# A fused attention and maxout kernel: the first weight pieces cut by column quarters, batch 1 loaded ahead of the weights, and zeros multiplied in the early waits of TensorE

## The chip, the cores and the metric

The kernel runs on one core of one Trainium2 chip. The metric is the device time of one execution in microseconds (us). The numbers used here are the median of the timed runs and the span, busy times and rows of one profiled execution.

## The reference

Two parts follow each other. In the first, tokens `x` (8 batches, 8 heads, 512 tokens, 64 wide) read a small state (32 rows for each batch and head) by softmax attention, and the state reads the tokens. In the second, the 544 result rows of each batch (all heads side by side, 512 wide) go through a maxout layer of width 1024 and back to 512.

```python
scores = scale * np.matmul(x, state.transpose(0, 1, 3, 2))      # scale = 1 / sqrt(64)
a = softmax(scores);   xread = np.matmul(a, state)
scores2 = scale * np.matmul(state, x.transpose(0, 1, 3, 2))
a2 = softmax(scores2); sread = np.matmul(a2, x)
x = concatenate([xread, sread], axis=2)   # rows of 512 = heads x 64
g = np.maximum(x @ w1, x @ w2)
return (g @ w_out).astype(np.float32)     # 4352 x 512
```

## The kernel before

The maxout is written as `max(h1, h2) = relu(h1 - h2) + h2`, so only two weight matrices are needed: `wd = W1 - W2` (512 x 1024) and `wwo = W2 @ Wo` (512 x 512). Since `xread` is attention times state, the state of a batch is multiplied into both first (`sw`), and the attention weights then work on the small products. All matmuls are in bf16. The output of a token block is `relu(at @ sw) @ Wo + at @ (state @ wwo)`.

The program has three stretches. A first stretch, written out by hand as a table of tokens (`ORDER`), loads everything that comes first, builds `wd` and `wwo`, and does batches 0 and 1 and the preparation of batch 2. A loop then does batches 2 to 6 and prepares the next one in each pass, and a tail does batch 7 and the rows of the state. A branch at the end, not taken for these inputs, holds a slower general form.

Each token of `ORDER` emits one helper's instructions, so the table fixes the order on every engine. The name stands for the helper; numbers are batch, half, piece or chunk; `@n` names the PSUM bank (there are eight), `>V`, `>A`, `>P` the engine: VectorE (DVE), ScalarE (ACT), GpSimd (POOL). Transfers are issued by SyncE's queue (SP), in the order of the table; only the first piece of the state goes through ScalarE's queue.

- `ldx.b.g` loads half of batch b's heads, `ldS` state, `ldw1.k` and `ldw2.k` piece k of W1 and W2 (512 KB each, `PIECES` gives its columns and rows), `ldwo.q` a quarter of Wo's rows (512 KB).
- `ce` casts a pair of heads to bf16 (L209), `xt` transposes half a batch on TensorE in 8 matmuls (L225), `xte` copies that out. `sc` is the scores (8 matmuls, L240), `exp` the exponential on ScalarE (L248), `red` the sums and their reciprocal, `mul` the normalised weights `a`, `at` their transpose (L267), `ate` its copy. `sr`, `sre`, `srt`, `srte` are the state's reading of the tokens (L280 to L299).
- `cS`, `S`, `Se` cast, transpose and copy the state of the first batches (`sbd`). `mS`, `Sd`, `cb`, `xtd`, `atd` do the same work for later batches with DMA transposes, which SyncE issues (L204, L218, L261).
- `cw2.k` casts a piece of W2, `w2.k` transposes it (8 matmuls, L405), `w2e.k` copies it out to `w2m`. `cwo.q` casts a quarter of Wo. `ww.i.q` adds two matmuls (L460) to row block i of `wwo`: it needs `w2e` of the columns 256q to 256q + 255 and `cwo.q`. `wwe.i` copies block i out.
- `sub.k.h` subtracts half a piece, giving `wd` (L417). `sw.b.z` multiplies the state of batch b into chunk z of `wd` (`CHUNKS`) or, for `w`, into `wwo`, 8 small matmuls into two banks (L309); `swe` copies each bank out.
- `l1.b.f` is one block of 128 of the 1024 columns, two matmuls (L332), `re` its relu. `l2.b.c.q` adds two matmuls of quarter q (L346), or of the state part for `o` (L341), to output chunk c; `le` copies the chunk out and `store` writes the batch.

`idle.9@0` puts nine matmuls of zeros (L426, tile `wz`) ahead of the first transposes. `RELEASE` is the order in which the loop takes the eight banks, six for one ring and two for the other. A token that uses a bank waits until the bank's last reader is done. Each engine works strictly in its own order.

Of the kernel before, what the change touches and what calls it, by code (L numbers as in the profile page):

```python
# [20 lines left out]
ORDER = """
ldx.0.0 ldS.0.1 idle.9@0 ldx.0.1 ldw2.2 ldw2.3 ldwo.3 ldw1.3 ldw1.2 ldS.1.2 ce.0.0>V ce.0.1>P ldx.1.1 cS.0.1>V ldx.1.0
S.0.1@0 xt.0.0@1 Se.0.1.0>V Se.0.1.1>A ce.0.2>P ce.0.3>A xte.0.0>V xt.0.1@0 ldwo.2 sc.0.0@1 xte.0.1>V exp.0.0>A
cw2.2>P ldw2.1 sc.0.1@0 red.0.0>V exp.0.1>A w2.2@1 mul.0.0>P cw2.3>A sr.0@0 red.0.1>V ldw2.0 mul.0.1>P sre.0>V w2.3@2
cwo.3>A ldwo.0 w2e.2>V srt.0@0 at.0.0@3 srte.0>A sub.3.0>V w2e.3>A ldwo.1 sub.3.1>V ldw1.0 ate.0.0>A ww.2.3@2
sub.2.0>V ldw1.1 at.0.1@1 cS.1.2>A ww.3.3@3 ww.1.3@0 sub.2.1>V ate.0.1>A ldS.2.8 S.1.2@4 sw.0.1@1,5 Se.1.2.1>V
ce.1.3>A Se.1.2.0>V ce.1.2>P sw.1.1@4,6 swe.0.1.1>V ww.0.3@7 swe.0.1.0>A swe.1.1.0>V xt.1.1@5 swe.1.1.1>A ce.1.1>P
l1.0.7@1 ce.1.0>A xte.1.1>V l1.0.4@6 l1.0.6@4 re.0.7>A re.0.4>V cwo.2>P xt.1.0@5 re.0.6>A sc.1.1@1 l1.0.5@6 xte.1.0>V  # L30
exp.1.1>A ww.3.2@3 re.0.5>A sc.1.0@1 red.1.1>V ww.1.2@0 exp.1.0>A ww.2.2@2 cw2.1>V ww.0.2@7 l2.0.1.2@1 mul.1.1>P
ldx.3.1 red.1.0>V w2.1@6 cw2.0>A l2.0.2.2@5 mul.1.0>P w2e.1>V l2.0.2.3@5 l2.0.1.3@1 cwo.0>V w2.0@6 at.1.1@4 ww.2.0@2
w2e.0>V ldx.2.1 ww.3.0@3 cwo.1>P ate.1.1>V ww.0.0@7 ww.1.0@0 sub.0.1>V ldx.2.0 ww.3.1@3 at.1.0@4 ldx.3.0 sub.0.0>V
ww.0.1@7 wwe.3>A ww.1.1@0 sub.1.1>P ate.1.0>V wwe.0>A ww.2.1@2 wwe.1>V l1.1.7@7 wwe.2>A sr.1@4 sub.1.0>V re.1.7>A
sw.0.w@2,0 sre.1>V sw.0.0@3,6 swe.0.w.1>A l1.1.5@7 swe.0.w.0>V l1.1.6@4 swe.0.0.1>A mS.1>P l1.1.4@0 re.1.5>A re.1.6>V
l2.0.0.2@6 re.1.4>A l2.0.1.o@1 swe.0.0.0>V ce.3.2>P sw.1.0@4,7 mS.0>A sw.1.w@3,0 ce.3.3>P swe.1.0.1>V l2.0.0.3@6
swe.1.w.1>A cb.3.1>P Sd l1.0.0@2 swe.1.0.0>V l1.0.1@7 swe.1.w.0>A re.0.0>V l2.0.3.2@4 cb.2.1>P re.0.1>A l2.0.2.o@5
l1.1.1@2 ce.3.0>P l2.0.1.0@1 re.1.1>V l1.0.2@7 cb.2.0>P l1.1.3@3 re.0.2>V l2.0.3.o@4 re.1.3>A ce.3.1>P xtd.2 l1.1.0@2
ce.2.1>P l2.0.3.0@4 re.1.0>A srt.1@3 l2.0.0.0@6 ldx.4.0 cb.3.0>P srte.1>V l1.0.3@2 l2.0.0.o@6 re.0.3>A ce.2.2>P
l2.0.3.3@4 xtd.3 l1.1.2@2 ce.2.0>P l2.0.1.1@1 re.1.2>A ce.2.3>P l2.1.3.2@3 le.0.1>V l2.1.3.3@3 l2.1.3.1@3 l2.1.3.0@3  # L40
l2.1.2.2@1 ldx.4.1 l2.1.0.o@2 sc.2.1@7 l2.0.3.1@4 exp.2.1>A sc.2.0@0 l2.0.0.1@6 exp.2.0>A red.2.1>V l2.1.0.0@2
le.0.3>A l2.1.0.3@2 red.2.0>V mul.2.1>P l2.1.0.2@2 l2.1.2.3@1 le.0.0>V l2.1.2.o@1 mul.2.0>P l2.1.0.1@2 l2.0.2.0@5
le.1.0>A atd.2 l2.1.2.1@1 l2.0.2.1@5 l2.1.3.o@3 le.0.2>A l2.1.2.0@1 le.1.3>V sw.2.1@5,2 store.0 le.1.2>A sw.2.0@6,4
swe.2.1.0>V sw.2.w@3,0 swe.2.1.1>A sr.2@1 swe.2.0.0>V l2.1.1.3@5 swe.2.w.1>A l2.1.1.o@5 sre.2>V swe.2.0.1>A l2.1.1.2@5
l2.1.1.1@5 swe.2.w.0>V srt.2@1 l2.1.1.0@5 srte.2>V le.1.1>A
"""
# [8 lines left out]
@with_exitstack
def kernel(
# [363 lines left out]
    def wo_cast(q, eng):  # L420
        copy(eng, wo[:, 2 * q:2 * q + 2, :], half("o", q // 2)[:, q % 2 * 2:q % 2 * 2 + 2, :])

    def idle(n, ring):
        p = bank(ring)
        for j in range(n):
            nc.tensor.matmul(p, wz[:, 0:128], wz, start=True, stop=True)  # L426
# [2 lines left out]
    nc.vector.memset(ones, 1.0)
# [244 lines left out]
```

## Time and profile before

| | us |
|---|---|
| median of 3 runs | 150.77 (150.74 to 151.8) |
| profiled execution, its own time | 150.94 |
| span of the profiled execution | 149.0 |
| TensorE busy in the span | 138.1 (93%) |
| VectorE, ScalarE, GpSimd busy | 83.3, 66.1, 53.0 |
| mean granted TensorE clock | 0.989 |

A row of the timeline gives start, duration, engine, line, operation, output and inputs, the number of merged instructions, and in brackets how long the engine had been idle and what ended that. Matmuls are pipelined, so a merged row's duration is longer than the distance to the next row's start; the price of a step is read from start to start. DMA rows show the issue on a queue (SPq), and the landing of a transfer shows in the first row that waited for it. Lines are those of the kernel before; in the changed kernel all lines from the table's end on are two higher.

### The profile page before, as it was taken

The page shows a single profiled execution, that of the slowest core. Times are in us where ns is not written, and L with a number is a line of the kernel's source. Part 1 is how long each engine was busy: PE and PEld are TensorE (multiplying, and loading weights), DVE is VectorE, ACT ScalarE, POOL GpSimd, SP SyncE. Part 2 cuts the span into 40 slices and gives each one's busy share as a digit, 9 for nine tenths or more (in the row PEclk, how much of TensorE's full clock was granted, in tenths as well). Part 3 has the DMA queues.
Part 4 walks back from the last instruction along what each step waited for, and adds up shares of the span by engine and source line. Part 5 has one row for each costly group of instructions (what it writes and reads, how often), then busy time and mean ns, then how long its engine had stood idle before and what let it go on. Part 6 is the DMA issues. An engine that isn't in the chain of part 4 may idle for free.

```text
span 149.0 us, 3067 instructions
## 1 busy us (share of the span) xinstructions
PE 138.1 (93%) x1205; PEld 68.9 (46%) x1224; DVE 83.3 (56%) x163; ACT 66.1 (44%) x120; POOL 53.0 (36%) x81
## 2 busy tenths in 40 slices
PE   6846979999999999999999999999999999999990
PEld 2435446434445445444544454454445344754460
DVE  3567876796415367583855485376637586640120
ACT  3258673387324557045632745181547135511100
POOL 4352147497913700735091437056500500000000
PEclk9987999999999999999999999999999999999999
DMA  4999999996996568986969598779306033302332
GB/s 137 255 396 362 370 387 378 283 342 93 189 246 200 106 248 297 129 208 230 235 145 290 234 114 189 264 282 145 70 31 255 7 66 141 145 0 96 115 140 80
DMA packets 36063, 29.44 MB, mean 198 GB/s; under 512 B 23120, under 2 KB 31568, under 8 KB 35152
## 3 DMA queue, kind: packets, MB, share of 16 engines
q1 hardware_dynamic: 35776, 29.17, 69.9%
q8 instruction: 10, 0.16, 0.4%
q10 hardware_dynamic: 272, 0.07, 0.2%
q14 instruction: 5, 0.04, 0.1%
HBM read 15.20 MB, written 8.91 MB: 162 GB/s over the span
## 4 chain that ended last, share of the span: by engine, by line
PE 81%; DMA 10%; SPq 3%; DVE 1%; issue 1%; POOL 1%; ACT 0%
PE bank L346 38%; PE bank L332 17%; PE bank L341 9%; DMA big<-in_moe_w_out_dram 7%; PE bank L309 4%; PE bank L460 3%; DMA big<-in_x_dram 3%; SPq L155 3%; PE bank L365 2%; PE bank L375 2%; PE bank L240 2%; PE bank L280 1%; PE bank L373 1%; DVE wd L417 1%; POOL wo L103 1%
## 5 line engine op out<-in xcount | busy, mean ns | idle before, releaser
L346 PE MATMUL bank<-wo,r 128*128 128x512 bf16 (+1 forms) x259 | 61.4, 372 | 0.5
L346 PEld LDWEIGHTS <-r 128*128 128x128 bf16 x264 | 25.4, 98 | 28.5 <-issue 0.3
L99 ACT COPY big<-bank 128x512 f32<-128x512 f32 (+1 forms) x17 | 9.7, 573 | 47.1 <-PE bank L346 47.1
L332 PE MATMUL bank<-at,sw 128*128 128x512 bf16 x126 | 30.0, 379 | 0.1
L256 POOL TENSOR_TENSOR a<-e,er 128x512 bf16<-128x512 bf16 x16 | 16.7, 1065 | 36.3 <-ACT e L248 16.0
L327 DVE TENSOR_SCALAR r<-bank 128x512 bf16<-128x512 f32 x29 | 20.0, 691 | 15.9 <-PE bank L332 15.5
L325 ACT ACTIVATE r<-bank 128x512 bf16<-128x512 f32 x35 | 21.2, 608 | 8.2 <-PE bank L332 8.0
L101 DVE CAST sw<-bank 128x512 bf16<-128x512 f32 x24 | 15.3, 685 | 9.4 <-PE bank L309 9.3
L103 POOL CAST xe<-big 128x512 bf16<-128x512 f32 x28 | 16.4, 620 | 10.0 <-DMA big<-in_x_dram 10.0
L332 PEld LDWEIGHTS <-sw 128*128 128x128 bf16 x128 | 12.0, 98 | 14.0 <-issue 0.2
L101 DVE COPY big<-bank 128x512 f32<-128x512 f32 (+1 forms) x16 | 10.5, 654 | 13.6 <-PE bank L346 11.2
L341 PE MATMUL bank<-sw,at 128*128 128x512 bf16 (+1 forms) x56 | 17.1, 372 | 0.3
L103 POOL CAST xb<-big 128x1024 bf16<-128x1024 f32 x12 | 12.3, 1041 | 12.1 <-issue 11.4
L252 DVE TENSOR_REDUCE sums<-e 128x16 f32<-128x512 bf16 x16 | 10.6, 664 | 4.5 <-ACT e L248 4.4
L99 ACT CAST sw<-bank 128x512 bf16<-128x512 f32 x24 | 12.7, 599 | 0.2
L248 ACT ACTIVATE e<-bank 128x512 bf16<-128x512 f32 x16 | 9.0, 595 | 4.9 <-PE bank L240 4.5
L460 PE MATMUL bank<-wo,w2m 128*128 128x512 bf16 x30 | 7.8, 379 | 1.9 <-ACT w2m L99 1.2
L341 PEld LDWEIGHTS <-at 128*128 128x128 bf16 x66 | 5.7, 97 | 5.3
L240 PEld LDWEIGHTS <-xt 128*128 128x128 bf16 x128 | 5.1, 98 | 2.6 <-DVE xt L101 0.7
L240 PE MATMUL bank<-sbd,xt 128*128 128x64 bf16 x128 | 5.5, 193 | 0.6 <-DVE xt L101 0.6
L309 PE MATMUL bank<-wd,sbd 64*32 64x512 bf16 x128 | 5.8, 382 | 0.3 <-DVE sbd L101 0.2
L101 DVE COPY w2m<-bank 128x1024 bf16<-128x1024 bf16 (+1 forms) x4 | 2.8, 689 | 5.1 <-PE bank L375 4.1
(71 smaller groups left out, 105.1 us busy)
## 6 DMA issues: line engine op xcount, KB each, us to landing
big<-in_x_dram SPq DMA_DIRECT2D x14, 512.0 KB, 5.1
out_dram<-big SPq DMA_DIRECT2D x7, 1024.0 KB, 6.0
big<-in_moe_w_dram SPq DMA_DIRECT2D x8, 512.0 KB, 10.2
...
```

The source lines that it names most:

```text
L99: nc.scalar.copy(o, i)
L101: nc.vector.tensor_copy(o, i)
L103: nc.gpsimd.tensor_copy(o, i)
L240: nc.tensor.matmul(pv[:, c, kk], xt_s[b % 2][:, c, k, :], sbd[:, b, k, :], start=(c == 0 and kk == 0), stop=(c == NC - 1 and kk == 1))
L256: (nc.gpsimd if eng == "P" else nc.vector).tensor_mul(e_view(a_s[b % 2], hh), e_view(e_s[b % 2], hh), er_s[b % 2][:, hh].unsqueeze(3).to_b ...
L309: nc.tensor.matmul(pg[g][32 * i:32 * i + 32, 0:n], sbd[64 * g:64 * g + 64, b, i, 32 * g:32 * g + 32], rhs, start=True, stop=True)
L325: nc.scalar.activation(out=o, in_=p, func=ACTF.Relu)
L327: nc.vector.tensor_scalar(o, p, scalar1=0.0, scalar2=None, op0=ALU.max)
L332: nc.tensor.matmul(p, sw_s[b % 3][:, g, f * 128:(f + 1) * 128], at_s[b % 3][:, g].rearrange("p c t -> p (c t)"), start=(g == 0), stop=(g = ...
L341: nc.tensor.matmul(p[:, lo:hi], at_s[b % 3][:, g, c, :], sw_s[b % 3][:, g, FF + lo:FF + hi], start=(start and g == 0), stop=(stop and g == 1))
L346: nc.tensor.matmul(p[:, lo:hi], r_s[b % 2][:, f, c * 128:(c + 1) * 128], wo[:, f, lo:hi], start=(start and j == 0), stop=(stop and j == le ...
L460: nc.tensor.matmul(p, w2t[:, f, i, :], wo[:, f, :], start=(first and f % 2 == 0), stop=(last and f % 2 == 1))
```

## The change

Four things change, and with them the whole table of the first stretch.

- `PIECES`: the first half of W1's and W2's columns is cut into two column quarters over all rows (256 columns, rows of 1 KB in DRAM) instead of two row halves over 512 columns (rows of 2 KB). The second half stays as it was. The second quarter (piece 1) is loaded first.
- `CHUNKS`: batch 0 multiplies its state into `wd` in three chunks (256, 256, 512) instead of two.
- Zeros: the nine of `idle.9` become 21 single matmuls of zeros (`fill.k`; 512 columns for k from 100 on, else 256), twelve ahead of the first transposes and nine between later steps.
- `RELEASE`: the loop takes the banks in another order.

```diff
-PIECES = [(0, 512, 0, 2), (0, 512, 2, 4), (512, 1024, 0, 2), (512, 1024, 2, 4)]
+PIECES = [(0, 256, 0, 4), (256, 512, 0, 4), (512, 1024, 0, 2), (512, 1024, 2, 4)]
-CHUNKS = [[(0, 512), (512, 1024)], [(0, 512), (512, 1024)]]
+CHUNKS = [[(0, 256), (256, 512), (512, 1024)], [(0, 512), (512, 1024)]]
 ORDER = """
-ldx.0.0 ldS.0.1 idle.9@0 ldx.0.1 ldw2.2 ldw2.3 ldwo.3 ldw1.3 ldw1.2 ldS.1.2 ce.0.0>V ce.0.1>P ldx.1.1 cS.0.1>V ldx.1.0
+ldx.0.0 ldS.0.1 fill.103@0 ldx.0.1 fill.106@1 ldS.1.2 fill.100@0 ldx.1.1 fill.111@1 ldx.1.0 fill.2@0 fill.13@1
...
-RELEASE = [7, 2, 6, 0, 4, 3, 1, 5]
+RELEASE = [2, 4, 6, 0, 3, 7, 5, 1]
...
-    def idle(n, ring):
+    def idle(n, ring, w=512):
         p = bank(ring)
         for j in range(n):
-            nc.tensor.matmul(p, wz[:, 0:128], wz, start=True, stop=True)
+            nc.tensor.matmul(p[:, 0:w], wz[:, 0:128], wz[:, 0:w], start=True, stop=True)
...
+        fill=lambda k, r: idle(1, r, 512 if k >= 100 else 256),
```

On SyncE's queue, at the program's start, the transfers stood in this order (`big` are ten buffers of 1 MB, `sf` is the state; batch 0 goes to `big0`, batch 1 to `big7`):

```order
L155 DMA big0_109<-in_x_dram 128x4x256 x2
L163 DMA big4_113<-in_moe_w2_dram 128x2x512 x2
L167 DMA big6_115<-in_moe_w_out_dram 128x2x512
L163 DMA big5_114<-in_moe_w1_dram 128x2x512 x2
L171 DMA sf0_81<-in_state_dram 128x2x64
L155 DMA big7_116<-in_x_dram 128x4x256 x2
L167 DMA big6_115<-in_moe_w_out_dram 128x2x512
L163 DMA big1_110<-in_moe_w2_dram 128x2x512 x2
L167 DMA big3_112<-in_moe_w_out_dram 128x2x512 x2
L163 DMA big2_111<-in_moe_w1_dram 128x2x512 x2
```

Now they stand so:

```order
L157 DMA big0_109<-in_x_dram 128x4x256 x2
L173 DMA sf0_81<-in_state_dram 128x2x64
L157 DMA big7_116<-in_x_dram 128x4x256 x2
L165 DMA big1_110<-in_moe_w2_dram 128x4x256
L165 DMA big2_111<-in_moe_w1_dram 128x4x256
L165 DMA big1_110<-in_moe_w2_dram 128x4x256
L165 DMA big4_113<-in_moe_w2_dram 128x2x512
L169 DMA big3_112<-in_moe_w_out_dram 128x2x512 x2
L165 DMA big2_111<-in_moe_w1_dram 128x4x256
L169 DMA big6_115<-in_moe_w_out_dram 128x2x512
L165 DMA big4_113<-in_moe_w2_dram 128x2x512
L169 DMA big6_115<-in_moe_w_out_dram 128x2x512
```

State and batch 1 moved ahead of all weights, W2's quarters of 256 columns come first among these, and the first piece of Wo (`big3`, here `wo.1`) moved from the third place of the weights to the fifth. W1's second half (`big5`), which was loaded early, now comes last, behind the rows shown.

On ScalarE's queue, from batch 0's second exponential on, stood before (`e` exponentials, `wb` and `wo` casts of weights, `w2m` the transposed W2, `at` transposed attention, `xe` casts of x, `sw` the chunk products):

```order
L248 ACTIVATE e0_91<-bank0_63 128x8x64
L99 CAST wb1_108<-big4_113 128x1024
L99 CAST wo0_77<-big6_115 128x1024
L99 COPY sread_t0_78<-bank0_63 128x4x32
L99 COPY w2m0_80<-bank2_65 128x4x256
L99 COPY at0_99<-bank3_66 128x512
L99 CAST sb0_82<-sf0_81 128x256
L99 COPY at0_99<-bank1_64 128x512
L99 CAST xe1_85<-big7_116 128x2x4x64
```

Now stands there, up to the copy out of bank 5, which the first `ww` step takes next:

```order
L250 ACTIVATE e0_91<-bank1_64 128x8x64
L101 CAST xe1_85<-big7_116 128x2x4x64
L101 COPY xt1_88<-bank3_66 128x4x256
L101 COPY xt1_88<-bank1_64 128x4x256
L250 ACTIVATE e1_92<-bank0_63 128x8x64
L250 ACTIVATE e1_92<-bank1_64 128x8x64
L101 COPY w2m0_80<-bank4_67 128x1024
L101 COPY at0_99<-bank0_63 128x512
L101 CAST sw0_102<-bank3_66 128x256
L101 CAST sw0_102<-bank4_67 128x256
L101 CAST wb0_107<-big4_113 128x1024
L101 COPY sread_t0_78<-bank5_68 128x4x32
```

Batch 1's copies and exponentials moved ahead of the first weight work, the copies of `xt` came over from VectorE, and the cast of the first Wo piece went from here to VectorE.

More of the change, by code (lines that the diff above doesn't have):

```diff
@@ L26 @@
[L26 to L45, printed above, removed]
+ldx.0.0 ldS.0.1 fill.103@0 ldx.0.1 fill.106@1 ldS.1.2 fill.100@0 ldx.1.1 fill.111@1 ldx.1.0 fill.2@0 fill.13@1
@@ new lines @@
+ldw1.3 sub.1.0>P fill.113@0 red.1.0>V sr.1@1 w2e.1>A at.0.1@0 at.0.0@2 ldS.2.8 cw2.0>P ate.0.1>A sre.1>V sw.0.1@4,3
+srt.0@5 fill.4@6 fill.10@7 swe.0.1.1>A ate.0.0>V mul.1.0>P swe.0.1.0>A w2.0@3 red.1.1>V cw2.3>A l1.0.2@4 srt.1@2
+l1.0.3@7 cwo.1>V srte.0>A w2.3@6 re.0.3>A mul.1.1>V ww.2.1@5 ww.0.1@1 cwo.0>P w2e.0>A srte.1>V at.1.1@7 ww.1.1@0
+re.0.2>V ww.3.1@2 ate.1.1>A at.1.0@4 sub.0.0>V ww.0.0@1 w2e.3>A ww.2.0@5 sub.0.1>V ww.3.0@2 ate.1.0>A ww.1.0@0 cwo.2>V
+sw.1.0@4,6 ldx.2.0 sw.0.0@7,3 ww.2.2@5 swe.1.0.1>A swe.1.0.0>V ww.3.2@2 swe.0.0.1>A cw2.2>V l1.1.0@4 l1.1.2@3
@@ new lines @@
+swe.0.0.0>V w2.2@6 cwo.3>A re.1.0>V ldx.2.1 l1.0.0@7 w2e.2>V l1.0.1@4 re.1.2>A ww.2.3@5 sub.2.0>V re.0.0>A l1.1.3@3
+ldx.3.1 ww.3.3@2 wwe.2>A re.0.1>V sub.2.1>P ww.0.3@1 ldx.3.0 wwe.3>A ww.0.2@1 sub.3.1>V ww.1.3@0 re.1.3>A ww.1.2@0
+sub.3.0>V wwe.0>A l1.1.1@3 mS.1>P wwe.1>A sw.0.2@1,2 re.1.1>V sw.1.1@4,5 swe.0.2.0>A sw.0.w@0,7 swe.0.2.1>V sw.1.w@3,6
+swe.1.1.1>A l2.0.0.0@1 swe.1.1.0>V l2.0.0.1@1 swe.0.w.0>A l1.0.7@5 swe.0.w.1>V mS.0>A l2.0.3.0@0 cb.2.0>P re.0.7>V
+l1.1.5@7 swe.1.w.1>A Sd l1.1.4@4 re.1.5>V ce.2.1>P l1.0.5@5 re.1.4>A l1.0.4@6 cb.2.1>P swe.1.w.0>V re.0.5>A l2.0.3.1@0
@@ L46 @@
+l2.0.0.3@1 l2.1.1.3@3 atd.2 le.0.0>A l2.0.1.0@6 le.1.1>A l2.1.2.1@7 le.0.1>V xtd.3 sw.2.w@1,4 le.1.2>A sw.2.1@3,5
+swe.2.w.0>V sw.2.0@6,0 swe.2.w.1>A sr.2@7 swe.2.0.0>V l2.1.0.0@1 swe.2.0.1>A l2.1.0.o@1 swe.2.1.0>A sre.2>V store.0
+l2.1.0.1@1 swe.2.1.1>A l2.1.0.2@1 l2.1.0.3@1 srt.2@5 srte.2>A le.1.0>V
 """
```

13 lines of the change are left out of this document (11 added, 2 removed).

## The prediction

> **What bounds the kernel now.** I read the page first (span, granted clock, chain of waits), then TensorE's rows in the timeline, then the busy time by stage, and last the rows of the other engines that a transfer released.
>
> ```profile
> span 149.0 us, 3067 instructions
> ...
> PEclk9987999999999999999999999999999999999999
> ...
> PE 81%; DMA 10%; SPq 3%; DVE 1%; issue 1%; POOL 1%; ACT 0%
> ```
>
> TensorE carries the chain for 81% of the span, DMA for 10%, some 15 us. The table by stage shows where TensorE begins to be full (columns: stage, its length, then PE, PEld, DVE, ACT, POOL busy, granted clock, DMA share, GB/s):
>
> ```profile
> 6.44:9.86 3.42, 1.71 (x28) 1.13 (x26) 2.62 (x5) 1.91 (x4) 1.12 (x2) 1.00 0.96 338
> 9.86:13.27 3.41, 3.04 (x53) 2.46 (x53) 1.95 (x7) 2.40 (x4) 2.33 (x3) 0.50 1.06 389
> 21.30:31.72 10.42, 10.25 (x114) 5.33 (x114) 8.25 (x17) 4.66 (x8) 6.47 (x5) 1.00 1.08 340
> 31.72:54.66 22.94, 22.70 (x184) 10.53 (x185) 12.14 (x25) 11.54 (x21) 12.87 (x17) 1.00 0.79 202
> ```
>
> From 21.30 us on TensorE is full: 10.25 of 10.42 and 22.70 of 22.94 us. What the change can win or lose therefore lies before 21.30. TensorE's rows there, and the rows from which I price its steps:
>
> ```profile
> 1.27 4.02 PE L426 MATMUL bank<-wz 128*128 128x512 bf16 x9 [1.27 <-DVE ones L429]
> ...
> 10.22 1.03 PE L405 MATMUL bank<-ident,wb 128*128 128x128 bf16 x8 [1.33 <-POOL wb L103]
> ...
> 14.54 0.38 PE L460 MATMUL bank<-wo,w2m 128*128 128x512 bf16 x1 [1.19 <-ACT w2m L99]
> ...
> 19.99 0.39 PE L240 MATMUL bank<-sbd,xt 128*128 128x64 bf16 x8
> 20.22 0.38 PE L332 MATMUL bank<-at,sw 128*128 128x512 bf16 x1
> 21.30 0.59 PE L460 MATMUL bank<-wo,w2m 128*128 128x512 bf16 x2 [0.70 <-POOL wo L103]
> ...
> 23.69 0.61 PE L405 MATMUL bank<-ident,wb 128*128 128x128 bf16 x8
> 24.14 1.46 PE L346 MATMUL bank<-wo,r 128*128 128x512 bf16 x6
> ...
> 30.30 0.43 PE L280 MATMUL bank<-xe,e 128*32 128x65 bf16 x32
> 30.66 0.41 PE L309 MATMUL bank<-wwo,sbd 64*32 64x512 bf16 x8
> ...
> 33.98 0.41 PE L309 MATMUL bank<-wd,sbd 64*32 64x512 bf16 x8
> ...
> 34.54 0.60 PE L346 MATMUL bank<-wo,r 128*128 128x512 bf16 x2
> ...
> 41.97 2.75 PE L346 MATMUL bank<-wo,r 128*128 128x512 bf16 x12
> 44.56 0.59 PE L341 MATMUL bank<-sw,at 128*128 128x512 bf16 x2
> ```
>
> Three waits stand out, each on a weight piece or its cast and copy: 1.33, 1.19 and 0.70 us. From start to start, twelve matmuls take 44.56 - 41.97 = 2.59, so a step of two (one `ww`, `l1` or `l2`) takes 0.43; a `w2` step 24.14 - 23.69 = 0.45; an `sr` step 30.66 - 30.30 = 0.36; an `sc` step 0.23; a pair of `sw` steps 34.54 - 33.98 = 0.56, so 0.28 each.
>
> The transfers, by the rows that a landing released (the releaser stands in brackets, and the row's start is the landing within some 0.1 us):
>
> ```profile
> 6.21 0.61 POOL L103 CAST xe<-big 128x512 bf16<-128x512 f32 x1 [0.82 <-DMA big<-in_x_dram]
> ...
> 9.13 1.04 POOL L103 CAST wb<-big 128x1024 bf16<-128x1024 f32 x1 [2.30 <-DMA big<-in_moe_w_dram]
> ...
> 14.67 1.29 DVE L417 TENSOR_TENSOR wd<-big,big 128x512 bf16<-128x512 f32 x2 [0.17 <-DMA big<-in_moe_w_dram]
> ...
> 16.29 0.62 ACT L99 CAST xe<-big 128x512 bf16<-128x512 f32 x1 [0.52 <-DMA big<-in_x_dram]
> ...
> 18.83 0.62 ACT L99 CAST xe<-big 128x512 bf16<-128x512 f32 x1 [0.94 <-DMA big<-in_x_dram]
> ...
> 20.21 1.04 POOL L103 CAST wo<-big 128x1024 bf16<-128x1024 f32 x1 [0.74 <-DMA big<-in_moe_w_out_dram]
> ...
> 28.50 1.26 POOL L417 TENSOR_TENSOR wd<-big,big 128x512 bf16<-128x512 f32 x1 [1.82 <-DMA big<-in_moe_w_dram]
> ```
>
> Six pieces of weights with rows of 2 KB land between 20.21 and 28.50, so 1.38 us each. The first one needs 9.13 - 6.21 = 2.92, a late start of 1.54. State piece and first half of batch 1, with rows of 1 KB, take 16.29 - 14.67 = 1.62; I put 1.5 on a piece with rows of 1 KB. The second half took 2.54, a straggle of 1.04.
>
> **The change, part by part.** *The balance.* I compare at the first `ww` step: `ww.2.1` in the new order, the wait that ends at 21.30 in the old. By then the new order has done one `sc`, one `w2`, one `sr` and one `srt` more (0.23 + 0.45 + 0.36 + about 0.1 = 1.14), and four `ww`, two `l1` and one `sw` less (6 x 0.43 + 0.28 = 2.86). The two orders are level if `ww.2.1` starts at 21.30 - (2.86 - 1.14) = 19.58. Every tenth earlier is won, every tenth later lost, as long as TensorE is full behind it.
>
> *What gates `ww.2.1`: transfers.* Batch 1 now comes ahead of all weights. Its halves land at 6.21 + 1.62 = 7.8 and 9.3 (10.4 with the straggle). Then come W2 and W1 of the second quarter and W2 of the first at 1.5 each, W2.3 and Wo.1 at 1.38. Without a late start `wo.1` lands at 9.3 + 4.5 + 2.76 = 16.6, with it at 18.1, with the straggle too at 19.2. I take 18.2, since the first weight piece showed the late start and no row excludes it in the new place; the straggle I leave to the range. `wo.1` is cast on VectorE, and the row for this cast is below: `ww.2.1` starts at 18.2 + 0.68 + 0.05 = 18.95.
>
> [...]
>
> *What gates `ww.2.1`: ScalarE.* In the new order it runs a queue that begins with batch 1's second half and ends with the copy that frees bank 5 for `ww.2.1`.
>
> ```profile
> 8.93 0.60 ACT L248 ACTIVATE e<-bank 128x512 bf16<-128x512 f32 x1 [0.39 <-PE bank L240]
> ...
> 10.43 1.05 ACT L99 CAST wb<-big 128x1024 bf16<-128x1024 f32 x1 [0.90 <-DMA big<-in_moe_w_dram]
> ...
> 12.97 0.45 ACT L99 COPY sread_t<-bank 128x128 bf16<-128x128 bf16 x1
> 13.15 1.11 ACT L99 COPY w2m<-bank 128x1024 bf16<-128x1024 bf16 x1
> ...
> 14.16 0.59 ACT L99 COPY at<-bank 128x512 bf16<-128x512 bf16 x1
> ...
> 14.79 0.41 ACT L99 CAST sb<-sf 128x256 bf16<-128x256 f32 x1
> ...
> 24.95 0.68 DVE L101 CAST wo<-big 128x1024 bf16<-128x1024 f32 x1
> ```
>
> One cast (0.62, row at 16.29), two copies of x (2 x 1.11), two exponentials (2 x 0.60), the copy of W2 (1.11), `ate` (0.59), two halves of `swe` (2 x 0.41, by the cast of the same width), the cast of W2 (1.05) and `srte` (0.45): 8.06 us. From 9.3 that ends at 17.4, from 10.4 at 18.5. With my landings it also waits some 0.8 for W2's first cast and for W2.3, so 18.3: 0.6 ahead of the transfers' path. ScalarE is late next; if the weights came early, it would hold the start between 17.4 and 18.5.
>
> *GpSimd's queue* casts `w2.1` (landed 12.3, by 13.4), subtracts (1.26, `w1.1` landed 13.8, by 15.1) and casts `w2.0` (landed 15.3, by 16.4), by its rows at 9.13 and 28.50. Each is done before the ScalarE or TensorE step that uses it in the sums above: hidden.
>
> *Behind `ww.2.1`.* From there to `sw.0.2` the new order has 16 `ww`, 6 `l1`, 2 `at`, 1 `w2` and 2 `sw` steps: 22 x 0.43 + 2 x 0.22 + 0.45 + 0.56 = 10.9 us, so TensorE is there at 29.9. The last weight lands by 28.50 + 4 x 0.12 = 29.0 (four pieces of 1 KB rows), and VectorE's two subtractions (0.65 each, half of the row at 14.67) end at 30.3, so TensorE waits 0.4. Then four `sw` steps follow each other and wait for banks to be copied out; I put 0.5 on that. The old stage lost 0.6 in such waits: its 17 steps of two, two `w2`, `at` and `sw`, one `sc` and `sr` make 9.8 of its 10.42 us. Net I charge 0.3.
>
> *Zeros.* Twelve of the 21 matmuls of zeros stand ahead of the first transposes, seven of 512 and five of 256 columns: at 4.02/9 = 0.45 for 512 about 4.2 us, as the nine before, and hidden under the first transfer. The other nine stand in front of steps that wait for VectorE, ScalarE or a landing; 0.11 to 0.22 each, hidden by waits of the size shown, 1.2 us in all if that cover were gone. None lies on a bank whose last reader the next real step need not wait for as well, so they add no wait of their own.
>
> *Finer chunks of batch 0.* One more `sw` step (0.28) and two evictions of 256 columns for one of 512 each: counted in the steps above.
>
> *The queue of SyncE.* The transpose of batch 3 now stands behind that of `at` for batch 2 instead of ahead of it:
>
> ```profile
> 49.38 1.24 SPq L261 DMA_TRANSPOSE at<-a  x1
> ...
> 58.12 0.63 PE L240 MATMUL bank<-sbd,xt 128*128 128x64 bf16 x16
> ```
>
> ```profile
> xt<-xb SPq DMA_TRANSPOSE x6, 6.8
> ```
>
> So it is issued at about 49.38 + 1.24 = 50.6 and lands, at the median of 6.8, at 57.4. Its first reader starts at 58.12. Hidden, with 0.7 to spare; I charge nothing, and at most 0.5. The new ring of banks changes names only.
>
> *The sum.* 18.95 - 19.58 = -0.63, +0.3 for the waits at the last weight: -0.35. The profiled execution took 150.94 us by its own clock (149.0 of it span), the median of the runs is 150.77: 150.6 against the one, **150.4** against the other.
>
> **The rivals.** *Weights too late (the other side).* Everything that feeds `ww` waits behind 1 MB of batch 1. With straggle, `wo.1` lands at 19.2 and `ww.2.1` starts at 19.95: 0.4 later than level, with the 0.3 behind it 151.4. With a second straggle of 1.04 (the extra row length hits one more piece) it is 152.5. It decides at a landing of 18.9; for it speaks that the old trace shows both delays, against it that they need not add. Chance 0.27.
>
> *TensorE starves less than I think.* No late start: `wo.1` at 16.6, ScalarE holds the start at about 18.0, and the last weight lands at 27.5, so the waits behind vanish: 19.58 - 18.0 = 1.6 won, 149.2; with half of it 149.9. For it speaks that x streams without a pause before the weights. Chance 0.2.
>
> *The zeros don't hold the clock.* In the old trace the clock fell to 0.50 from 9.86 to 13.27 after a stage in which TensorE was busy 1.71 of 3.42 us. If such a stage of 3.41 us falls on full work after `ww.2.1`, half of it is lost, 1.7 us: 152.1; if it falls before, 0.5 at most: 150.9. The new order has as sparse a stage between 6.5 and 13, with two batches' transposes and scores in it, but full work begins only near 19. Chance 0.1 for the first price; the second lies inside my forecast.
>
> [...]
>
> *The transpose of batch 3 comes late:* up to 0.5 us, 150.9, chance 0.03.
>
> **How the numbers follow.** My own case, 0.4: `ww.2.1` between 18.3 and 19.5, so 149.8 to 151.0, and 150.4 in the middle. A measurement of this kernel can tell about 1% from no change, 149.26 to 152.28. Faster by more: over half of the second rival, 0.12. Slower by more: the upper half of the first rival and a third of the third, with 0.04 for what no row shows, 0.21. The rest, 0.67, is within 1%. The range from 149.2 to 152.2 takes in the level start, both rivals' first prices and leaves 2 in 10 out.
>
> **What would show it.** Right: the first row of L462 (`ww`, two lines lower now) starts near 18.95 and was released by VectorE's cast of `wo`; from there on TensorE shows no wait over 0.4. The clock stays at 1.00 from 6.5 on. Wrong: `wo.1` landing after 18.9, a ScalarE row as the releaser, waits between 20 and 30, or a granted clock of 0.50 behind 17; a wait at `sc` of batch 3 would show SyncE's queue.

## The result, and the profile after

| | before | after | forecast |
|---|---|---|---|
| median of 20 runs each, us | 151.03 (149.54 to 151.8) | 150.17 (149.9 to 151.03) | 150.4 |
| ratio, with its 95% interval | 1 | 0.9952 (0.9934 to 0.9969) | |
| profiled execution, us | 150.94 | 149.99 | 150.6 |
| span, us | 149.0 | 148.2 | |
| first `ww` step starts, us | | 18.84 | 18.95 |
| loop's first `l1` starts, us | 54.66 | 53.79 | |

The changed kernel is faster by 0.5%, about 0.7 us; the interval lies wholly below 1, but the gain is less than the 1% that the prediction's chances went by. These lines of the page answer to those shown of before (span, granted clock in 40 slices, the chain of waits by engine):

```profile
span 148.2 us, 3127 instructions
...
PEclk9999999999999999999999999999999999999998
...
PE 84%; DMA 6%; SPq 5%; DVE 1%; issue 1%; ACT 0%; DVEq 0%
```

DMA's share of the chain fell from 10% to 6% (that of SyncE's queue rose from 3% to 5%), and the clock no longer dips in the first slices. The table by stage (start and end of the stage, its length, then PE, PEld, DVE, ACT and POOL busy, granted clock, DMA share, GB/s) has its cuts at the first `ww`, at the first `l2` and at the start of the loop's first `l1`:

```profile
5.30:18.84 13.54, 10.35 (x188) 7.33 (x186) 11.20 (x25) 10.44 (x19) 7.38 (x7) 1.00 1.07 356
18.84:31.16 12.32, 12.23 (x109) 5.65 (x109) 10.17 (x17) 9.07 (x16) 4.33 (x3) 1.00 1.10 350
31.16:53.79 22.63, 22.60 (x177) 10.56 (x170) 9.77 (x19) 10.34 (x19) 13.17 (x17) 1.00 0.70 160
53.79:148.20 94.41, 90.38 (x770) 44.17 (x768) 49.78 (x97) 37.35 (x72) 25.39 (x32) 0.99 0.56 166
```

TensorE is full from 18.84 on (12.23 of 12.32 us, then 22.60 of 22.63); before it was full from 21.30 on, with 2.86 - 1.14 us more work already done, of a total that is one `sw` step smaller. From the loop on nothing changed: 148.20 - 53.79 = 94.41 us, against 149.0 - 54.66 = 94.34 before. So the whole difference lies in the first stretch, as the prediction had it. TensorE's rows there:

```profile
9.72 0.62 PE L227 MATMUL bank<-ident,xe 128*128 128x128 bf16 x8 [0.93 <-POOL xe L105]
10.97 0.62 PE L227 MATMUL bank<-ident,xe 128*128 128x128 bf16 x8 [0.64 <-POOL xe L105]
...
13.43 0.62 PE L407 MATMUL bank<-ident,wb 128*128 128x128 bf16 x8 [0.25 <-POOL wb L105]
...
17.87 0.61 PE L407 MATMUL bank<-ident,wb 128*128 128x128 bf16 x8
18.84 1.04 PE L462 MATMUL bank<-wo,w2m 128*128 128x512 bf16 x4 [0.36 <-DVE wo L103]
...
29.37 0.59 PE L334 MATMUL bank<-at,sw 128*128 128x512 bf16 x2
29.89 0.62 PE L311 MATMUL bank<-wd,sbd 64*32 64x512 bf16 x16
...
31.16 1.04 PE L348 MATMUL bank<-wo,r 128*128 128x512 bf16 x4
```

Row L462 is the step that the prediction rests on: `ww.2.1` starts at 18.84, 0.36 us late, and waited for VectorE's cast of `wo`. The longest waits now stand at batch 1's transposes (0.93 and 0.64), where x is late; those at the weights' transposes and at `ww` shrank from 1.33, 1.19 and 0.70 to 0.25 and 0.36. The rows that a landing released, on VectorE, GpSimd and ScalarE (the first two are batch 1's halves, then `w1.1`, `w2.0`, `wo.1`, `w1.3`):

```profile
8.77 0.43 DVE L103 CAST xe<-big 128x512 bf16<-128x512 f32 x1 [0.32 <-DMA big<-in_x_dram]
...
13.35 1.80 DVE L419 TENSOR_TENSOR wd<-big,big 128x512 bf16<-128x512 f32 x1 [0.28 <-DMA big<-in_moe_w_dram]
...
18.09 0.69 DVE L103 CAST wo<-big 128x1024 bf16<-128x1024 f32 x1 [0.31 <-DMA big<-in_moe_w_out_dram]
...
27.90 1.52 DVE L419 TENSOR_TENSOR wd<-big,big 128x512 bf16<-128x512 f32 x2 [0.15 <-DMA big<-in_moe_w_dram]
```

```profile
10.30 0.61 POOL L105 CAST xe<-big 128x512 bf16<-128x512 f32 x1 [0.64 <-DMA big<-in_x_dram]
...
14.81 1.24 POOL L105 CAST wb<-big 128x1024 bf16<-128x1024 f32 x1 [0.20 <-DMA big<-in_moe_w_dram]
```

```profile
17.14 0.44 ACT L101 COPY sread_t<-bank 128x128 bf16<-128x128 bf16 x1
```

The first four are VectorE's: VectorE began to wait for `wo.1` at 17.78 and got it at 18.09. The last row is the end of ScalarE's queue ahead of `ww.2.1`, at 17.58: half a microsecond ahead of the landing.

### The profile page after: what moved, and what is told of

Read it like the earlier page. It is cut to its first block, busy times and chain, and to the rows that moved or that the text cites. A ratio compares the mean times of both kernels' runs of the same rounds, so it can differ in the third digit from the quotient of the medians.

```text
span 148.2 us, 3127 instructions
## 1 busy us (share of the span) xinstructions
PE 139.6 (94%) x1244; PEld 69.5 (47%) x1244; DVE 82.7 (56%) x161; ACT 69.3 (47%) x127; POOL 51.8 (35%) x78
## 4 chain that ended last, share of the span: by engine, by line
PE 84%; DMA 6%; SPq 5%; DVE 1%; issue 1%; ACT 0%; DVEq 0%
PE bank L348 37%; PE bank L334 18%; PE bank L343 10%; DMA big<-in_moe_w_out_dram 6%; PE bank L462 5%; PE bank L311 4%; SPq L165 3%; PE bank L367 2%; PE bank L377 2%; PE bank L242 2%; PE bank L282 1%; SPq L157 1%; PE bank L375 1%; DVE wo L103 0%; DVE r L329 0%
## 5 line engine op out<-in xcount | busy, mean ns | idle before, releaser
L329 DVE TENSOR_SCALAR r<-bank 128x512 bf16<-128x512 f32 x32 | 22.1, 692 | 16.1 <-PE bank L334 15.6
L258 POOL TENSOR_TENSOR a<-e,er 128x512 bf16<-128x512 bf16 x14 | 14.5, 1050 | 34.8 <-DVE er L255 19.4
L327 ACT ACTIVATE r<-bank 128x512 bf16<-128x512 f32 x32 | 19.3, 609 | 10.0 <-PE bank L334 9.8
L103 DVE CAST sw<-bank 128x512 bf16<-128x512 f32 (+1 forms) x23 | 14.4, 673 | 9.3 <-PE bank L311 9.3
L343 PE MATMUL bank<-sw,at 128*128 128x512 bf16 (+1 forms) x66 | 19.1, 373 | 0.0
L105 POOL CAST xe<-big 128x512 bf16<-128x512 f32 x26 | 15.2, 623 | 7.2 <-DMA big<-in_x_dram 7.2
L101 ACT CAST sw<-bank 128x512 bf16<-128x512 f32 (+1 forms) x27 | 13.6, 578 | 1.4 <-PE bank L311 1.4
L462 PE MATMUL bank<-wo,w2m 128*128 128x512 bf16 x32 | 7.9, 380 | 0.4 <-DVE wo L103 0.4
L428 PE MATMUL bank<-wz 128*128 128x256 bf16 (+1 forms) x21 | 6.5, 438 | 1.3 <-DVE ones L431 1.3
L419 DVE TENSOR_TENSOR wd<-big,big 128x512 bf16<-128x512 f32 x6 | 5.3, 912 | 1.2 <-DMA big<-in_moe_w_dram 1.2
L101 ACT COPY w2m<-bank 128x1024 bf16<-128x1024 bf16 (+1 forms) x4 | 3.6, 906 | 4.9 <-PE bank L377 4.6
```

Source lines behind the costliest of these rows:

```text
L101: nc.scalar.copy(o, i)
L103: nc.vector.tensor_copy(o, i)
L105: nc.gpsimd.tensor_copy(o, i)
L258: (nc.gpsimd if eng == "P" else nc.vector).tensor_mul(e_view(a_s[b % 2], hh), e_view(e_s[b % 2], hh), er_s[b % 2][:, hh].unsqueeze(3).to_b ...
L327: nc.scalar.activation(out=o, in_=p, func=ACTF.Relu)
L329: nc.vector.tensor_scalar(o, p, scalar1=0.0, scalar2=None, op0=ALU.max)
```

## The experiments

The theory: the landing of `wo.1` sets the start of the first `ww` step, behind it TensorE is full, so the time follows that landing; the zeros and the ring do nothing for the time. The rivals: the gain comes from the clock, which the zeros hold up; it comes from the ring of the loop; it comes from loading batch 1 early whatever the order behind; a still earlier `wo.1` would give still more. Lines of the diffs are pieces of `ORDER`, with a neighbour on each side.

### e1: without the zeros between later steps

```diff
-Se.0.1.1>A fill.0@3 S.1.2@4 fill.15@1 xte.0.1>V
+Se.0.1.1>A S.1.2@4 xte.0.1>V
-Se.1.2.1>A fill.110@1 ldwo.0
+Se.1.2.1>A ldwo.0
-mul.0.1>V fill.5@3 fill.6@2 sc.1.1@0
+mul.0.1>V sc.1.1@0
-cw2.1>P fill.14@2 sre.0>V
+cw2.1>P sre.0>V
-sub.1.0>P fill.113@0 red.1.0>V
+sub.1.0>P red.1.0>V
-srt.0@5 fill.4@6 fill.10@7 swe.0.1.1>A
+srt.0@5 swe.0.1.1>A
```

> The changed kernel without the nine single matmuls of zeros between steps; the twelve ahead of the first transposes stay. Transfer theory (the landing of wo.1 sets the first ww step, and with it the time): the zeros only filled waits, so the first ww step starts within 0.2 us of the changed kernel's 18.84 and the time is within 0.3 us of the changed kernel's, 0.5 to 1.0 us under the kernel before. Clock theory (the gain came from zeros that held the granted clock): the clock falls to 0.50 for 3.4 us somewhere between 8 and 17 us, the copies and transposes behind it come later, and half or more of the 0.8 us is lost.

Measured: 150.33, ratio to before 0.9971 (0.9942 to 1.0). The clock fell, for one stretch of 3.42 us (same columns as above):

```profile
7.80:11.24 3.44, 1.98 (x42) 1.47 (x43) 3.31 (x8) 2.76 (x5) 2.20 (x3) 1.00 1.09 353
11.24:14.66 3.42, 3.29 (x90) 2.59 (x90) 3.11 (x5) 2.83 (x5) 3.22 (x4) 0.50 1.08 359
```

```profile
13.10 1.03 PE L406 MATMUL bank<-ident,wb 128*128 128x128 bf16 x8
...
19.15 1.04 PE L461 MATMUL bank<-wo,w2m 128*128 128x512 bf16 x4 [1.01 <-DVE wo L102]
```

In the slow stretch eight transposes of W2 took 1.03 us instead of 0.62 (row at 13.43 of the changed kernel), and the wait for `wo.1` swallowed it: TensorE still stood idle for 1.01 us before `ww.2.1`. The first `ww` comes 0.31 later than with the zeros, outside the 0.2 that was expected; this belongs to the cast's row, which waited for its transfer until 18.39 instead of 18.09. Of e1's 12 runs five have a mean clock of 0.989 or less, of the changed kernel's 20 three. So without the nine late zeros the clock seems to fall there more often, and a held clock is worth nothing here: the median of e1's five runs is 150.35, that of its other seven 150.29. The fall lies where TensorE waits for transfers anyway.

### e2: no zeros at all

The edit is that of e1, and the twelve `fill` ahead of `xt.0.0` are gone too:

```diff
-ldx.0.0 ldS.0.1 fill.103@0 ldx.0.1 fill.106@1 ldS.1.2 fill.100@0 ldx.1.1 fill.111@1 ldx.1.0 fill.2@0 fill.13@1
+ldx.0.0 ldS.0.1 ldx.0.1 ldS.1.2 ldx.1.1 ldx.1.0
...
```

> The changed kernel without any of the 21 matmuls of zeros. Transfer theory: batch 0's transposes and scores run at half clock a little longer, but they end well before wo.1 lands, so again within 0.4 us of the changed kernel. Clock theory: TensorE stays at half clock until after 10 us and the first ww step starts 0.5 us or more later, so the time is at or over that of the kernel before.

Measured: 150.26, ratio 0.9962 (0.9936 to 0.9989). TensorE is slow at first and comes out level:

```profile
5.06 1.03 PE L225 MATMUL bank<-ident,xe 128*128 128x128 bf16 x8 [5.06 <-DVE xe L101]
...
9.40 1.84 PE L225 MATMUL bank<-ident,xe 128*128 128x128 bf16 x16
...
13.06 0.62 PE L405 MATMUL bank<-ident,wb 128*128 128x128 bf16 x8 [0.16 <-POOL wb L103]
...
17.79 1.01 ACT L99 COPY w2m<-bank 128x1024 bf16<-128x1024 bf16 x1
...
18.08 0.69 DVE L101 CAST wo<-big 128x1024 bf16<-128x1024 f32 x1 [1.80 <-DMA big<-in_moe_w_out_dram]
...
18.83 1.04 PE L460 MATMUL bank<-wo,w2m 128*128 128x512 bf16 x4 [1.13 <-ACT w2m L99]
...
53.78 3.62 PE L332 MATMUL bank<-at,sw 128*128 128x512 bf16 x16
```

Up to 11 us eight transposes take 0.9 to 1.03 us, from 13 on 0.62, and yet `ww.2.1` starts at 18.83 and the loop at 53.78, within 0.01 us of the changed kernel. The zeros, all 21 of them, are worth nothing in this order. The bracket of the `ww` row names ScalarE's copy, which ended at 18.80, only 0.03 behind the cast of `wo` (18.08 + 0.69 = 18.77). That copy (`w2e.0`) isn't an input of `ww.2.1`; in the changed kernel it runs from 18.57, and the step starts at 18.84, before it ends. So the landing of `wo.1` at 18.08 sets the start here too. The granted clock on record can't tell of the slow beginning: it stands at 1.00 from 4 to 12 us of this profile, where eight transposes take 0.9 to 1.03, and none of the 12 runs has a mean under 0.994.

### e3: `wo.1` one transfer later

The two loads of Wo pieces change places; nothing else.

```diff
-xte.0.0>V ldwo.1 Se.0.1.1>A
+xte.0.0>V ldwo.0 Se.0.1.1>A
-fill.110@1 ldwo.0 exp.0.0>A
+fill.110@1 ldwo.1 exp.0.0>A
```

> The changed kernel with the loads of wo.1 and wo.0 exchanged, so wo.1 lands one piece (1.35 us) later and nothing else moves. Transfer theory: the first ww step starts at 20.2 instead of 18.84, TensorE is full behind it, so the time rises by 1.1 to 1.4 us over the changed kernel, some 0.4 us above the kernel before. Rival (ScalarE's queue and the copies hold TensorE as much as the landing does, or waits further back absorb the delay): a rise of under 0.5 us.

Measured: 151.83, ratio 1.0069 (1.003 to 1.0107), but the twelve runs fall into two groups: seven at 151.27 to 151.86 and five at 153.31 to 153.98. The profiled execution is of the upper group:

```profile
20.19 1.89 PE L462 MATMUL bank<-wo,w2m 128*128 128x512 bf16 x4 [2.34 <-DVE wo L103]
...
57.04 3.19 PE L334 MATMUL bank<-at,sw 128*128 128x512 bf16 x14
```

```profile
16.70:20.14 3.44, 1.16 (x13) 0.68 (x10) 1.12 (x4) 1.75 (x3) 1.04 (x1) 1.00 1.07 370
20.14:23.55 3.41, 3.36 (x11) 1.46 (x12) 3.26 (x6) 1.01 (x2) 0.00 (x0) 0.50 1.06 387
```

The first `ww` starts at 20.19, 1.35 later than in the changed kernel, which is one transfer of 1.38; the lower group's median is 1.4 above the changed kernel's 150.17. That is the theory's size. The upper group is a second thing: in the stretch with the wait of 2.34 us for `wo.1` TensorE was busy 1.16 of 3.44 us, behind it the clock was halved, and the halved stretch of 3.41 us fell on full work. From the first `ww` to the loop it took 57.04 - 20.19 = 36.85 us instead of 34.95, 1.9 more. It is the prediction's third rival, with its price of 1.7, but only when `wo.1` is late.

### e4: Wo's pieces ahead of W2.3

```diff
-ce.0.2>A ldw2.3 Se.0.1.0>V
+ce.0.2>A Se.0.1.0>V
-ldwo.0 exp.0.0>A
+ldwo.0 ldw2.3 exp.0.0>A
...
-red.1.1>V cw2.3>A l1.0.2@4
+red.1.1>V l1.0.2@4
-srte.0>A w2.3@6 re.0.3>A
+srte.0>A re.0.3>A
-ate.1.1>A at.1.0@4 sub.0.0>V
+ate.1.1>A cw2.3>A at.1.0@4 w2.3@6 sub.0.0>V
```

> The changed kernel with wo.1 and wo.0 loaded ahead of W2.3, and W2.3's cast and transposes moved behind the ww steps of quarter 1. Transfer theory: wo.1 lands near 16.7, the first ww step starts when TensorE is through with l1.0.3, near 17.9, and has one w2 step (0.45) less behind it: 0.94 - 0.45 = 0.5 us faster than the changed kernel, unless W1.3's landing near 27.9 now makes TensorE wait, which leaves 0.3. Rival (ScalarE's queue or the last weight is the real bound): no gain, within 0.2 us.

Measured: 150.42, ratio 0.996 (0.9939 to 0.9981), level with the changed kernel.

```profile
18.27 1.04 PE L462 MATMUL bank<-wo,w2m 128*128 128x512 bf16 x4 [0.35 <-DVE wo L103]
...
21.16 0.62 PE L407 MATMUL bank<-ident,wb 128*128 128x128 bf16 x8 [0.54 <-ACT wb L101]
...
54.38 3.62 PE L334 MATMUL bank<-at,sw 128*128 128x512 bf16 x16
```

```profile
17.59 0.63 DVE L103 CAST wo<-big 128x1024 bf16<-128x1024 f32 x1
```

`ww.2.1` is 0.57 earlier and the loop 0.59 later. The cast's row has no bracket: the piece was there, and VectorE still had the sums of batch 1 to do, so the landing no longer gates. What was put behind (W2.3) is waited for at 21.16, and its transposes, 0.45 us, now stand behind the first `ww`: from there to the loop it takes 36.11 us instead of 34.95, TensorE idle for 0.71 of them instead of 0.12. This profiled execution (150.78) was 0.36 above the kernel's median, so the typical loss behind `ww` may be smaller. The gain of 0.3 to 0.5 that was expected did not come, and the rival holds: an earlier `wo.1` alone buys nothing.

### e5: the kernel before, with zeros in its waits

Zeros alone added to the order before; it computes the same.

```diff
-sc.0.1@0 red.0.0>V
+sc.0.1@0 idle.5@2 red.0.0>V
-at.0.0@3 srte.0>A
+at.0.0@3 idle.5@4 srte.0>A
```

> The kernel before with five matmuls of zeros in each of its two longest waits (behind sc.0.1 and behind at.0.0), nothing else moved. Clock theory: the stage at 0.50 between 9.86 and 13.27 is gone, and the time falls by half or more of the 0.8 us that the whole change brought. Transfer theory: the w2 and at steps run at full clock, but TensorE's wait that ends at 21.30 still ends on the cast of wo.2, which lands at 20.2 as before, so the time is within 0.2 us of the kernel before.

Measured: 151.0, ratio 0.9979 (0.9953 to 1.0005). In its profile the clock still fell, from 8.69 to 12.10, and the wait for Wo remained, 0.50 for the 0.70 of before:

```profile
8.69:12.10 3.41, 3.41 (x33) 1.83 (x34) 1.77 (x4) 1.88 (x3) 2.89 (x3) 0.50 1.05 401
```

```profile
21.33 0.59 PE L460 MATMUL bank<-wo,w2m 128*128 128x512 bf16 x2 [0.50 <-POOL wo L103]
```

Ten zeros did not hold the clock in the profiled execution, but in most others they did: 11 of the 12 runs have a mean clock of 0.993 or more, against 2 of the 17 of the kernel before beside them. Those 11 have a median of 150.98, the 17 one of 151.06. The runs of the kernel before say the same. Of the 88 runs of the kernel before that stood beside the experiments, 59 had a mean clock up to 0.977 and a median of 151.1; 11 had 0.995 or more, no halved stretch to speak of, and a median of 151.03. A full clock is worth 0.1 us or less there, where the clock theory asked for 0.4 or more. It falls.

### e6: the kernel before, with batch 1 loaded first

```diff
-ldx.0.1 ldw2.2
+ldx.0.1 ldS.1.2 ldx.1.1 ldx.1.0 ldw2.2
-ldw1.2 ldS.1.2 ce.0.0>V
+ldw1.2 ce.0.0>V
-ce.0.1>P ldx.1.1 cS.0.1>V ldx.1.0 S.0.1@0
+ce.0.1>P cS.0.1>V S.0.1@0
```

> The kernel before with its state piece and batch 1 loaded ahead of the weights, as in the changed kernel, but with its own order of steps and its own pieces. The landings of wo.2 and of all later pieces stay. Transfer theory with the balance: W2.2 lands near 12 instead of 9.1, the w2, sub, ww and sw steps that stand ahead of batch 1's steps in TensorE's order come 3 us later, and batch 1's data wait unused; TensorE is through with them some 1 to 3 us later, so slower by 1 to 3 us: the early load pays only with the order that uses it. Rival (the early load of batch 1 is the gain by itself): faster by 0.3 us or more.

Measured: 153.36, ratio 1.0148 (1.0115 to 1.0181).

```profile
12.31 1.03 PE L405 MATMUL bank<-ident,wb 128*128 128x128 bf16 x8 [3.35 <-POOL wb L103]
```

```profile
9.53:19.77 10.24, 6.10 (x72) 3.99 (x73) 4.80 (x11) 5.34 (x9) 5.21 (x6) 0.50 1.04 383
```

TensorE, which wants W2 next in the old order, stands still for 3.35 us, and the clock stays at 0.50 for 10.24 us, three times the 3.41 of a single fall. With the old order and the old pieces, loading batch 1 early loses 2.3 us; how much of that is the wait and how much the halved clock, this run doesn't separate. The change also puts batch 1's transposes and scores into the time that the early load costs. The two go together.

### e7: the old ring in the loop

```diff
-RELEASE = [2, 4, 6, 0, 3, 7, 5, 1]
+RELEASE = [7, 2, 6, 0, 4, 3, 1, 5]
```

> The changed kernel with the ring of banks (RELEASE) of the kernel before. Theory that the ring changes names only: within 0.2 us of the changed kernel. Rival (the old ring meets banks whose readers are late at the start of the loop, near 53.8 us): 0.2 to 0.8 us slower, with waits at the first l1 steps of batch 2.

Measured: 150.21, ratio 0.9936 (0.9915 to 0.9956); the changed kernel has 150.17.

```profile
19.12 1.04 PE L462 MATMUL bank<-wo,w2m 128*128 128x512 bf16 x4 [1.25 <-DVE wo L103]
...
54.06 3.62 PE L334 MATMUL bank<-at,sw 128*128 128x512 bf16 x16
```

The loop starts 54.06 - 19.12 = 34.94 us after the first `ww`, as before the edit (34.95), and from the loop on it takes 148.5 - 54.06 = 94.44. The ring changes nothing. This profile's 0.28 later `ww` is again its later landing of `wo.1`, 18.37 for 18.09: over the profiles of kernels that issue the same transfers (the changed kernel, e1, e2, e7) it lies between 18.08 and 18.39.

### e8, e10 and e11: is the upper group of e3 the clock?

e8 is e3 with eight zeros of 512 columns in the long wait; they compute nothing that is used. e10 repeats e3, and e11 repeats e8, both on one chip and in the same rounds.

```diff
-mul.1.1>V ww.2.1@5
+mul.1.1>V idle.8@5 ww.2.1@5
```

> The kernel with wo.1 one piece later, plus eight matmuls of zeros (1.7 us at full clock) in the wait of TensorE just ahead of the first ww step. In that kernel's profile the wait of 2.3 us was followed by a granted clock of 0.50 from 20.14 to 23.55, on full work. Clock theory, for this place: the zeros hold the clock, the first ww step still starts near 20.2, no stage of 0.50 falls on full work, and all runs lie near 151.5, none near 153.5. Rival (the clock falls for another reason, or the zeros delay the ww step): runs near 153.5 stay, or all runs are 0.3 us or more above 151.6.

> The kernel with wo.1 one piece later again, now beside the one with eight zeros in its long wait. [...] Rival (the upper group was an accident of that time): one group near 151.6.

> The same with the eight zeros in the wait, beside the run without them. Clock theory: no run near 153.5. If its lower group is level with that of the kernel without zeros, the 0.7 us between the two earlier runs was the chip or the day; if it stays 0.4 us or more above, the zeros themselves cost time.

Measured: e8 152.34, ratio 1.0096 (1.0073 to 1.012); e10 151.83, 1.0068 (1.003 to 1.0106), with three of its 12 runs in an upper group, where e3 had five of 12; e11 152.22, 1.0086 (1.0057 to 1.0115). The profile of e11:

```profile
17.68 1.89 PE L428 MATMUL bank<-wz 128*128 128x512 bf16 x8
20.53 1.02 PE L462 MATMUL bank<-wo,w2m 128*128 128x512 bf16 x4 [0.96 <-DVE wo L103]
```

and the two stages of e10's profiled execution, again one of the upper group:

```profile
17.90:21.39 3.49, 1.55 (x17) 0.91 (x15) 1.80 (x4) 1.50 (x2) 1.04 (x1) 1.00 1.07 373
21.39:24.80 3.41, 3.41 (x15) 1.56 (x13) 2.16 (x4) 2.09 (x3) 0.00 (x0) 0.50 1.06 389
```

The runs of the four kernels together, with the mean granted clock of each run:

| | runs | median, us | mean clock |
|---|---|---|---|
| no zeros in the wait (e3, e10), lower group | 16 | 151.71 | 0.995 to 1.0 |
| no zeros in the wait (e3, e10), upper group | 8 | 153.50 | 0.983 to 0.989 |
| eight zeros in the wait (e8, e11) | 17 | 152.22 (151.77 to 152.92) | 0.981 to 1.0, 15 of them 0.993 or more |

One stretch of 3.41 us at half clock lowers the mean over 151 us by 1.71 / 151 = 0.011, to 0.989. Every run above 153 has a clock of 0.989 or less, and no run of the lower group is under 0.995: the upper group is a halved stretch on full work. With the zeros the group is gone (none of 17, against 8 of 24), so they do hold the clock in this wait. They don't pay for themselves: the mean of the 17 is 152.28, that of the 24 is 152.30. Against the lower group they cost 0.5 us. Some 0.2 of it can be seen in the profiles, as a later first `ww` (20.37 and 20.53 against 20.19 and 20.34); the zeros end before `wo.1` is cast, so they don't stand in its way on TensorE. From `ww` to the loop e8 and e11 take 34.93 us, as the changed kernel does (34.95). What else these two profiles are longer by stands at the very end: from the issue of the last stores to the end of the span it is 5.8 and 6.2 us, against 5.5 in the changed kernel, e3 and e10. The lower group was never profiled, and the cause stays open. The expectation that all runs with zeros lie near 151.5 failed, and its rival (0.3 or more above 151.6) came true.

### e9: only `wo.1` ahead of W2.3, with the steps behind set for it

```diff
-ce.0.2>A ldw2.3 Se.0.1.0>V
+ce.0.2>A Se.0.1.0>V
-xte.0.0>V ldwo.1 Se.0.1.1>A
+xte.0.0>V ldwo.1 ldw2.3 Se.0.1.1>A
-w2.0@3 red.1.1>V cw2.3>A l1.0.2@4
+w2.0@3 cwo.1>V red.1.1>V l1.0.2@4
-l1.0.3@7 cwo.1>V srte.0>A w2.3@6 re.0.3>A mul.1.1>V ww.2.1@5 ww.0.1@1 cwo.0>P
+l1.0.3@7 srte.0>A re.0.3>A mul.1.1>V cw2.3>P ww.2.1@5 ww.0.1@1 ww.1.1@0 w2.3@6 cwo.0>P
-at.1.1@7 ww.1.1@0 re.0.2>V
+at.1.1@7 re.0.2>V
```

> A version after the fourth run's profile: wo.1 alone is loaded ahead of W2.3, its cast stands ahead of batch 1's second sum on VectorE, W2.3 is cast on GpSimd instead of ScalarE, and transposed behind three ww steps. Theory: the first ww step starts near 17.9, W2.3's cast ends near 19.1 before TensorE comes to it, and the later waits (the landings of W1.0, wo.2 and wo.3) take back half: 0.2 to 0.4 us faster than the changed kernel, 0.6 to 0.7% under the kernel before. Rival (the landings behind, not the first one, hold TensorE): within 0.1 us of the changed kernel.

Measured: 150.19, ratio 0.9948 (0.9932 to 0.9964); level with the changed kernel.

```profile
18.01 1.47 PE L462 MATMUL bank<-wo,w2m 128*128 128x512 bf16 x6 [0.68 <-ACT r L327]
19.86 0.62 PE L407 MATMUL bank<-ident,wb 128*128 128x128 bf16 x8 [0.38 <-POOL wb L105]
...
54.26 3.62 PE L334 MATMUL bank<-at,sw 128*128 128x512 bf16 x16
```

```profile
18.77 1.04 POOL L105 CAST wb<-big 128x1024 bf16<-128x1024 f32 x1 [2.02 <-DMA big<-in_moe_w_dram]
```

The `ww` steps begin 0.83 earlier, in front of a W2.3 that lands at 18.77. (The bracket names ScalarE's relu, which ended at 17.96; VectorE's cast of `wo` ended 0.01 before it.) As in e4, the loop starts no earlier (54.26), and the 0.2 to 0.4 us that were expected did not come. In both, the piece that was put back holds TensorE (0.54 and 0.38), and its transposes come on top. No version here beat the changed kernel.

## Why the prediction was right, and which sizes were off

The time lies in the range, and the path is the one that was forecast: TensorE full behind the first `ww`, and that step set by the landing of `wo.1`. The size of the gain is not: forecast 0.35, measured 0.7 (ratio) to 0.86 (difference of the medians). That 150.17 lies so close to 150.4 is in part luck, since the median of the kernel before rose from 150.77, in 3 runs, to 151.03, in 20.

- *The balance at the first `ww`: the start right, one term of the level left out.* `ww.2.1` was forecast at 18.95 and started at 18.84, released by VectorE's cast of `wo`. But the level of 19.58 counts one `sw` step as moved behind this point, and the finer chunks add one more: from there on the old table has seven `sw` steps and the new one nine. The prediction says that this step is counted, and in the level it isn't. At 0.28 (so much the step of 256 columns takes too, from 15.15 to the next row at 15.43) level is 19.58 - 0.28 = 19.30, and 0.46 was won at the first `ww`. With this term the prediction's sum would have been 18.95 - 19.30 + 0.3 = -0.05, no gain to speak of; it came near because this slip and the one at the last weight, below, go opposite ways. That is luck.
- *What the runs show of the path.* e3 moves the first `ww` by 1.35 and the lower group's time by 1.4 to 1.6. e2 leaves both alone. In e1 and e7 the start is 0.3 later in the profile and so is the end of that execution (150.3 and 150.28 for 149.99), while the medians are level. The rivals that don't pass through this landing, zeros and clock (e1, e2, e5) and ring (e7), are ruled out as the gain. No run takes the column quarters of `PIECES` or the chunks out alone, so their share of it is not shown.
- *The landings, right in their sum, wrong in one place.* The late start of 1.54 was put at the first weight piece. It came a transfer earlier: batch 1's first half landed at 8.77 instead of 7.8, and the second at 10.3 instead of 9.3; the first three weight pieces then took 14.81 - 10.30 = 4.51 us, 1.5 each as forecast. W2.3 and `wo.1` took 18.09 - 14.81 = 3.28 for a forecast of 2.76. Together `wo.1` was cast at 18.09 for a forecast landing of 18.2. The sum held partly by luck: two delays of 0.5 to 1.0 stood where one of 1.54 had been put. The 1.62 us behind the forecast of 1.5 also hold 64 KB of state: at the pace of 1.38 for 512 KB these are 0.17 of the 0.24 by which 1.62 exceeds 1.38, most of it, so that row alone was weak ground for 1.5.
- *ScalarE's queue, over-priced.* It began at 10.27 and ended at 17.58, 7.31 us with its waits where 9.0 had been put (9.3 to 18.3). The order of the two gates was right, the distance between them too small by half.
- *The zeros and the ring, right.* Hidden and of no use (e2), names only (e7).
- *The waits at the last weight, the term that was mis-sized most.* The prediction charged +0.3 net: the last weight at 29.0, subtracted by 30.3, a wait of 0.4, then four `sw` steps in a row. Measured: the last weight's row starts at 27.90, its two subtractions end at 29.42, and TensorE came to `sw.0.2` at 29.89 without a wait of more than 0.1. The stage from the first `ww` was forecast to reach that step in 10.9 us and took 29.89 - 18.84 = 11.05; the four `sw` steps took 31.16 - 29.89 = 1.27, 0.15 more than 4 x 0.28, where 0.5 had been put on their waits. The error was in the working: 29.0 was taken from the row of before (28.50 and four longer pieces), although the prediction's own `wo.1` at 18.2 with seven pieces behind it, six of 1.38 and one of 1.5, gives 28.0. The measured pace was (27.90 - 18.09) / 7 = 1.40 a piece. So nothing was lost behind the first `ww`, and 0.41 was won there: the loop starts 0.87 earlier (53.79 - 54.66), 0.46 of it from before. TensorE's idle time explains 0.29: between the first `ww` and the loop it is 0.09 + 0.03 us now, and was 0.17 + 0.24 behind 21.30. The other 0.12 stays open. From the loop on the new span is 0.07 longer, which makes the 0.8 between the two.
- *SyncE's queue, right.* The transpose of batch 3 stands behind that of `at`, and the loop's first scores come without a wait:

```profile
48.88 1.25 SPq L263 DMA_TRANSPOSE at<-a  x1
50.22 2.12 SPq L220 DMA_TRANSPOSE xt<-xb  x1
```

```profile
53.79 3.62 PE L334 MATMUL bank<-at,sw 128*128 128x512 bf16 x16
57.24 0.63 PE L242 MATMUL bank<-sbd,xt 128*128 128x64 bf16 x16
```

- *The rivals.* "Weights too late" did not occur in the change; e3 is that case made on purpose, and its lower group lies at 151.6, the rival's 151.4 with a first `ww` 0.24 later than the rival's 19.95. "Zeros don't hold the clock" had the right price, 1.7 for a measured 1.8, but its condition was not met in the change: a halved stretch on full work was seen only behind a wait of 1.94 (e10) and 2.34 us (e3) right in front of the first `ww`. With waits of 0.36 (the change), 1.01 (e1), 1.13 (e2, without any zeros) and 1.25 (e7) there was none in the profiles, and none of the runs of e2 and e7 is above 151.32.
